# Opening the gated unit by single tiles of tokens: one bank for both turned tiles, groups closed late, gate weights from a second queue

## The chip, the cores and the metric

The kernel runs on one core of a Trainium2 chip. The engines named here are TensorE (PE, with its weight loads listed apart as PEld), VectorE (DVE), ScalarE (ACT), GpSimd (POOL) and SyncE (SP), which in this kernel only issues transfers. The metric is the device time of one execution in microseconds: 184.51 us, the median of three runs (184.46 to 184.68).

## What is computed

The input is 2048 tokens of 448 values, in bfloat16. Each token is normalised over its 448 values. The normalised tokens go two ways.

```
xn   = (x - mean) / sqrt(var + 1e-5)
Bu   = xn @ B_bar^T                       # complex, 448 states
h[t] = Lam_bar * h[t-1] + Bu[t]           # complex recurrence over the tokens
s    = 2 * Re(h @ C^T) + xn * Dskip
g    = silu((sigmoid(xn @ w_gate) * (xn @ w_up)) @ w_down)      # 448 -> 1792 -> 448
out  = x + s * g
```

`B_bar` comes from `Lambda`, `log_dt` and `B`; `w_gate` and `w_up` are 448 x 1792, `w_down` is 1792 x 448.

## The kernel before

The tokens are cut into four chunks of 512 (`TC`), each of four tiles of 128 (`P`); `HC` is 256, half a chunk. The 448 inputs are held transposed in `xnT`, as three whole blocks of 128 rows and a last block of 64. That last block is stored twice, in rows 0 to 63 and 64 to 127, so that the last 64 rows of a gate product and of an up product can run side by side in the two halves of TensorE's rows. The 1792 columns of gate and up are 14 groups of 128 (`ft` 0 to 13). A group of a chunk is a sum of three whole products and one half product, in one PSUM bank for the gate (`g_ps`) and one for up (`u_ps`). The helper `gu_wholes` issues the whole products, `gu_halves` the half ones, over the tokens `n0` to `n1`; `first` says whether these products open the sum or close it.

There are eight PSUM banks. They are given out in turn under one tag (`bank`, 8 buffers): a new tile gets the oldest bank and has to wait until that one's last reader is done.

Chunk 0 is special, since nothing can run before its tokens are there (lines 929 to 1021). TensorE first runs 31 products on a unit matrix (`warm`). VectorE takes the statistics of tiles 0, 1 and 3, ScalarE those of tile 2. POOL takes the power -0.5 of the variance, VectorE normalises (`ln_norm`), a small copy doubles the last 64 columns (VectorE for tiles 0 and 1, POOL for 2 and 3), TensorE turns the tile by four transposes into PSUM (`ln_turn`, line 274), and VectorE copies the turned tile into `xnT` (`ln_out`, line 282). Tiles 0 and 2 are turned into one bank (`tps[0]`), tiles 1 and 3 into another (`tps[1]`).

The opening then takes the first four groups (`gus`) in two halves of the chunk. When tiles 0 and 1 are in `xnT`, the whole gate products of groups 0 to 2 are issued over 256 tokens, then their up products. Tiles 2 and 3 are turned. Then come the half products of groups 0 to 2 for the first 256 tokens, all of group 3 for those tokens, the half products of all four groups for the second 256 tokens, and at last their whole products, group by group. Group 3 uses the two banks of the turned tiles, and so waits for their copies. Between all this VectorE and ScalarE make the tables of sines and cosines for the recurrence (`emit_frac`, `emit_abs`, `emit_sin`, `emit_cos`); then ScalarE takes the tanh of each gate bank (`gu_out`) and VectorE copies each up bank (`up_copy`).

Behind the opening the main stream begins: groups 4 to 13 of chunk 0 and the products of the recurrence's input, and then the other chunks. All of its products are issued by one helper (`Sum.add`, line 510). `keep_order`, called at the end, ties each instruction to the one written before it on its engine: every engine runs its instructions in the order in which the code writes them.

Loads: SP issues nearly all transfers, in written order. At the start these are three loads of tokens of chunk 0 (tile 0, tile 1, tiles 2 and 3 together), then by `load_w(sync, 0, 512)` the first 512 columns of the gate weights, of the up weights, and of the last 64 rows of both (`wt`); then B, more weights and the tokens of chunk 1. ScalarE's queue issues three small rows of vectors before ScalarE's first table load.

Of the kernel before, what the change touches and what calls it, by code (L numbers as in the profile page):

```python
# [11 lines left out]
BF16 = mybir.dt.bfloat16  # L12
# [7 lines left out]
P = 128  # L20
TC = 512
HC = TC // 2
NCH = S_TOK // TC
TPC = TC // P
KT = 4
# [38 lines left out]
def kernel(  # L64
# [52 lines left out]
        eng.dma_start(out=t[:, 0:3, f0:f1], in_=mat[0:384, f0:f1].rearrange("(kt p) f -> p kt f", p=P))  # L117
        eng.dma_start(out=t[0:64, 3, f0:f1], in_=mat[384:448, f0:f1])

    def load_w(eng, f0, f1, between=None):  # L120
        for t, mat in ((wg, B_w_gate), (wu, B_w_up)):
            eng.dma_start(out=t[:, :, f0:f1], in_=mat[0:384, f0:f1].rearrange("(kt p) f -> p kt f", p=P))
        if between:
            between()
        for mat, p0 in ((B_w_gate, 0), (B_w_up, 64)):
            eng.dma_start(out=wt[p0:p0 + 64, f0:f1], in_=mat[384:448, f0:f1])
# [12 lines left out]
    load_row(act, 1, A_Lambda_im)  # L139
    load_row(act, 2, A_Lambda_re)  # L140
    sync.dma_start(out=x_t[0][:, 2:4, :], in_=x_src[:, 2:4, :])
    load_w(sync, 0, 512)
    raw = {}

    def load_x(c):
# [44 lines left out]
    def warm(n):  # L190
        for _ in range(n):
            pe.matmul(warm_ps[:], lhsT=ident[:], rhs=ident[:], start=True, stop=True)
# [74 lines left out]
    def ln_turn(c, j):  # L267
        xb, cols = xn[c % 3], slice(j * P, (j + 1) * P)
        if c > 0:
            sync.dma_start_transpose(out=xnT[c][:, 0:KT, cols], in_=xb[:, j, :])  # L270
            return
        (dve if j < 2 else pool).tensor_copy(out=xb[:, j, D:DP], in_=xb[:, j, 384:D])
        for kt in range(KT):
            pe.transpose(tps[j % 2][:, kt, :], xb[:, j, kt * P:(kt + 1) * P], ident[:])

    def ln_twice(c, copy, j0=0, j1=TPC):
        copy(out=xn[c % 3][:, j0:j1, D:DP], in_=xn[c % 3][:, j0:j1, 384:D])
# [1 line left out]
            ln_turn(c, j)  # L279

    def ln_out(j):
        dve.tensor_copy(out=xnT[0][:, :, j * P:(j + 1) * P], in_=tps[j % 2][:])  # L282

# [403 lines left out]

    def gu_halves(c, ft, gt, ut, first, n0=0, n1=TC):
        f0, f1 = ft * P, (ft + 1) * P
        for t, p0 in ((gt, 0), (ut, 64)):
            pe.matmul(t[:, n0:n1], lhsT=wt[p0:p0 + 64, f0:f1],  # L695
                      rhs=xnT[c][p0:p0 + 64, 3, n0:n1], start=first, stop=not first)

    def gu_wholes(c, ft, gt, ut, first, n0=0, n1=TC, which=(0, 1)):
        f0, f1 = ft * P, (ft + 1) * P
        for t, wm in [((gt, wg), (ut, wu))[i] for i in which]:  # L700
            for kt in range(3):
                pe.matmul(t[:, n0:n1], lhsT=wm[:, kt, f0:f1], rhs=xnT[c][:, kt, n0:n1],  # L702
                          start=(first and kt == 0), stop=(not first and kt == 2))


    def gu_out(ft, gt, ub):
# [229 lines left out]
    ln_root(1, 1)  # L936
    ln_sum(2)
    turn_twice(tp_v, rows, 3)
    tps = [ps.tile([P, KT, P], BF16, name="tp_x", tag="bank", bufs=8) for _ in range(2)]
    ln_norm(0, 0)  # L940
    ln_turn(0, 0)
    emit_vecs()
# [4 lines left out]
    ln_pow_of(2, 1, sums[:, 2:3, 1:2], 1.0 / D)  # L947
    ln_norm(0, 1)
    ln_turn(0, 1)
    warm(5)  # L950
    ln_out(0)
    ln_out(1)
    ln_stats(3)
# [5 lines left out]
    ln_pow_of(3, 1, mv[:, 3:4, 1:2], 1.0)  # L959

    gus = [(bank("g_ps"), bank("u_ps")) for _ in range(3)]
    for ft in range(3):
        gu_wholes(0, ft, *gus[ft], True, 0, HC, (0,))
    for ft in range(3):
        gu_wholes(0, ft, *gus[ft], True, 0, HC, (1,))
    ln_norm(0, 2)
    ln_turn(0, 2)
    emit_frac(0)
    ln_norm(0, 3)
    ln_turn(0, 3)  # L970
    emit_abs(0)
    for j in (2, 3):
        ln_out(j)
    emit_frac(1)
    emit_abs(1)
    emit_frac(3)
    emit_abs(3)
    emit_frac(2)
    emit_abs(2)
    for ft in range(3):  # L980
        gu_halves(0, ft, *gus[ft], False, 0, HC)
    gus.append((bank("g_ps"), bank("u_ps")))
    gu_wholes(0, 3, *gus[3], True, 0, HC)
    gu_halves(0, 3, *gus[3], False, 0, HC)
    for ft in range(4):
        gu_halves(0, ft, *gus[ft], True, HC, TC)
    for ft in range(4):
        gu_wholes(0, ft, *gus[ft], False, HC, TC)
    emit_steps()
    for pt in (0, 1, 3):  # L990
        emit_sin(pt)
# [152 lines left out]
```

## Time and profile before

| | |
|---|---|
| median of three runs | 184.51 us (184.46 to 184.68) |
| profiled execution, its own time | 184.13 us |
| its span, first to last instruction | 182.4 us |
| PE busy | 177.3 us, 97% of the span |
| DVE, ACT, POOL busy | 163.7, 113.7, 25.0 us |
| PE's warm-up products | 1.35 to 4.84 us |
| first gate product of chunk 0 | 6.73 us |
| first product of the main stream (L510) | 13.86 us |

Times in the profile's lines are microseconds from the start of the span. A line of the timeline gives start, length, engine, source line, operation, what it writes and reads, and how many instructions are put together; where an engine stood idle before, a bracket says for how long and what ended it. A line of the chain gives start, length and what held the end of the program there. PEld rows are weight loads, which overlap products. An engine name with a q, as SPq, is its sequencer, which issues transfers. Matmuls are pipelined, so the length of one row holds its latency, and the spacing of starts is what a product costs in a row of them.

### The profile page before, as it was taken

The page shows a single profiled execution, that of the slowest core. Times are in us where ns is not written, and L with a number is a line of the kernel's source. Part 1 is how long each engine was busy: PE and PEld are TensorE (multiplying, and loading weights), DVE is VectorE, ACT ScalarE, POOL GpSimd, SP SyncE. Part 2 cuts the span into 40 slices and gives each one's busy share as a digit, 9 for nine tenths or more (in the row PEclk, how much of TensorE's full clock was granted, in tenths as well). Part 3 has the DMA queues.
Part 4 walks back from the last instruction along what each step waited for, and adds up shares of the span by engine and source line. Part 5 has one row for each costly group of instructions (what it writes and reads, how often), then busy time and mean ns, then how long its engine had stood idle before and what let it go on. Part 6 is the DMA issues. An engine that isn't in the chain of part 4 may idle for free.

```text
span 182.4 us, 4465 instructions
## 1 busy us (share of the span) xinstructions
PE 177.3 (97%) x1701; PEld 104.0 (57%) x1701; DVE 163.7 (90%) x335; ACT 113.7 (62%) x236; POOL 25.0 (14%) x61
## 2 busy tenths in 40 slices
PE   7999999999999999999999999999999999999992
PEld 7776888446654445645654445545665545656552
DVE  4899999799989979999999999699999999699574
ACT  3999677978587787988277665067048657152220
POOL 4768557220000000004000000000000000000000
PEclk9999999999999999999999999999999999999999
DMA  5999997894434113011231010030000000011102
GB/s 154 321 321 276 214 132 120 267 288 97 90 79 86 32 29 101 5 59 43 59 61 29 4 29 0 4 101 0 4 14 16 4 16 15 4 53 51 29 25 76
DMA packets 27659, 15.07 MB, mean 83 GB/s; under 512 B 16243, under 2 KB 27638, under 8 KB 27638
## 3 DMA queue, kind: packets, MB, share of 16 engines
q1 hardware_dynamic: 27632, 14.79, 34.4%
q8 instruction: 13, 0.21, 0.5%
q14 instruction: 8, 0.07, 0.1%
q10 hardware_dynamic: 6, 0.00, 0.0%
HBM read 8.49 MB, written 1.84 MB: 57 GB/s over the span
## 4 chain that ended last, share of the span: by engine, by line
PE 94%; DVE 3%; DMA 1%; POOL 0%; issue 0%; DVEq 0%
PE g_ps L510 25%; PE d_ps L510 23%; PE u_ps L510 19%; PE bu L510 12%; PE y_ps L510 11%; PE g_ps L702 2%; PE u_ps L702 1%; DMA x<-in_A_x_dram 1%; DVE sg L861 1%; PE g_ps L695 1%; DVE xnT L282 0%; DVE xn L261 0%; DVE stats L208 0%; DVE o_l L867 0%; POOL rsd L238 0%
## 5 line engine op out<-in xcount | busy, mean ns | idle before, releaser
L510 PE MATMUL u_ps<-xnT,wu 64*128 64x512 bf16 x312 | 69.1, 376 | 0.0
L510 PE MATMUL g_ps<-xnT,wg 64*128 64x512 bf16 x312 | 61.8, 376 | 0.0
L740 ACT ACTIVATE sig<-g_ps 128x512 bf16<-128x512 f32 x52 | 29.1, 596 | 29.1 <-PE g_ps L510 29.1
L510 PE MATMUL bu<-xnT,bT 64*128 64x512 bf16 x196 | 45.7, 376 | 0.0
L510 PE MATMUL d_ps<-wd,hF 64*128 64x448 bf16 x448 | 43.9, 349 | 0.0
L510 PEld LDWEIGHTS <-hF 64*128 64x128 bf16 x448 | 26.5, 94 | 16.2
L510 PEld LDWEIGHTS <-wu 64*128 64x128 bf16 x312 | 25.8, 94 | 16.7 <-POOLq L512 1.6
L510 PEld LDWEIGHTS <-wg 64*128 64x128 bf16 x312 | 23.1, 94 | 16.3 <-POOLq L512 1.9
L740 ACT CAST ub<-u_ps 128x512 bf16<-128x512 f32 x52 | 29.3, 604 | 0.8 <-DVE hF L712 0.8
L510 PE MATMUL y_ps<-ct,h 64*128 64x448 bf16 (+2 forms) x203 | 22.8, 343 | 0.0
L510 PEld LDWEIGHTS <-bT 64*128 64x128 bf16 x196 | 17.8, 94 | 8.8
L589 DVE TENSOR_TENSOR_SCAN wv<-r_col,st,ta 128x512 bf16<-128x512 f32 x18 | 22.6, 1274 | 0.1
L737 DVE TENSOR_TENSOR hF<-sig,ub 128x512 bf16<-128x512 bf16 x52 | 20.8, 415 | 1.0 <-ACT ub L740 0.8
L510 PE MATMUL g_ps<-xnT,wt 64*128 64x512 bf16 x52 | 19.6, 376 | 0.0
L510 PE MATMUL u_ps<-xnT,wt 64*128 64x512 bf16 x52 | 19.6, 376 | 0.0
L510 PEld LDWEIGHTS <-h 64*128 64x128 bf16 (+1 forms) x203 | 13.3, 95 | 8.2 <-issue 0.4
L570 ACT CAST bus<-bu 128x512 bf16<-128x512 f32 x24 | 14.3, 596 | 2.1 <-PE bu L510 1.9
L768 ACT ACTIVATE sigd<-d_ps 128x448 bf16<-128x448 f32 x12 | 6.6, 549 | 12.3 <-PE d_ps L510 12.3
L238 POOL TENSOR_TENSOR rsd<-ve,mhalf 128x1 f32<-128x1 f32 (+2 forms) x8 | 7.3, 917 | 48.5 <-PE u_ps L510 45.6
L510 PEld LDWEIGHTS <-wt 64*128 64x128 bf16 x104 | 9.8, 94 | 4.9
L832 DVE TENSOR_TENSOR o_t<-y_ps,xn 128x448 bf16<-128x448 f32 x12 | 6.9, 618 | 3.7 <-PE y_ps L510 3.7
L583 DVE TENSOR_TENSOR ta<-ta,tb 128x1024 bf16<-128x1024 bf16 x12 | 8.3, 690 | 0.3
(151 smaller groups left out, 214.7 us busy)
## 6 DMA issues: line engine op xcount, KB each, us to landing
wd<-in_B_w_down_dram SPq DMA_DIRECT2D x1, 1568.0 KB, 7.4
x<-in_A_x_dram SPq DMA_DIRECT2D x3, 448.0 KB, 5.9
out_dram<-o_t SPq DMA_DIRECT2D x6, 224.0 KB, 2.1
wg<-in_B_w_gate_dram SPq DMA_DIRECT2D x2, 384.0 KB, 4.2
wu<-in_B_w_up_dram SPq DMA_DIRECT2D x2, 384.0 KB, 5.3
wg<-in_B_w_gate_dram SPq DMA_DIRECT2D x1, 576.0 KB
wu<-in_B_w_up_dram SPq DMA_DIRECT2D x1, 576.0 KB, 8.0
bsw<-bus SPq DMA_DIRECT2D x8, 64.0 KB, 2.1
```

What stands on the lines that cost most here:

```text
L238: pool.tensor_tensor(out=rsd[:, t:t + n, :], in0=ve[:, t:t + n, :], in1=mhalf[:, 0:n, :], op=ALU.pow)
L510: m = pe.matmul(self.t[:, n0:n1], lhsT=lhsT, rhs=rhs, start=self.done == 1, stop=self.done == self.n)
L570: empty = [lambda cc=cc: act.copy(out=bus[:, cc, :], in_=pst[cc][:]) for cc in range(2)]
L583: dve.tensor_tensor(out=T["ta"][:], in0=T["ta"][:], in1=T["tb"][:], op=add)
L589: dve.tensor_tensor_scan(out=T["wv"][:, cc, :], data0=rb, data1=T["ta"][:, cc, :], initial=(0.0 if c == 0 else st[pt][:, cc, :]), op0=mul, ...
L695: pe.matmul(t[:, n0:n1], lhsT=wt[p0:p0 + 64, f0:f1], rhs=xnT[c][p0:p0 + 64, 3, n0:n1], start=first, stop=not first)
L702: pe.matmul(t[:, n0:n1], lhsT=wm[:, kt, f0:f1], rhs=xnT[c][:, kt, n0:n1], start=(first and kt == 0), stop=(not first and kt == 2))
L737: dve.tensor_tensor(out=h[:], in0=sig[:], in1=ub[:], op=ALU.mult)
L740: u.empty = [lambda: act.activation(sig[:], gt[:], ACT.Sigmoid), lambda: act.copy(out=ub[:], in_=ut[:])]
L768: act.activation(sigd[:], ds[j][:], ACT.Sigmoid)
L832: dve.tensor_tensor(out=o[:, i, :], in0=ys[c, j + 2 * i][:], in1=xb[:, i, :], op=ALU.add)
L861: dve.tensor_tensor(out=sg[:, d0:d1], in0=ys[c, j][:, d0:d1], in1=gs[c][:, j, d0:d1], op=ALU.mult)
```

## The change

- The two turned tiles share one PSUM tile `tps`, one half each, where there were two tiles and two banks.
- The helpers no longer take `first`. A list `opened` remembers which banks have had a product: the first product in a bank opens it (`start`), and only the products marked `last` close it (`stop`).
- The gate products of groups 0 to 2 over the first 256 tokens are issued as two rounds of 128 tokens, tile 0 and then tile 1. The up products stay at 256.
- The gate products of group 3 over the first 256 tokens come ahead of the turn of tile 2, in a bank taken before; the half products of groups 0 to 2 come between the turns of tiles 2 and 3.
- The whole products over tiles 2 and 3 of groups 0 to 2 are issued in 128 tokens each: tile 2 directly behind the turn of tile 3, tile 3 at the end. Group 3's up products over the first 256 tokens follow those of tile 2.
- On VectorE one `emit_frac` moves between the copies of tiles 2 and 3.
- Two of the five warm-up products ahead of the first gate product are left out.
- The first load of gate weights is issued by ScalarE's queue (`first=act`), ahead of ScalarE's first table load.

```diff
--- before.py
+++ after.py
@@ -117,9 +117,9 @@
         eng.dma_start(out=t[:, 0:3, f0:f1], in_=mat[0:384, f0:f1].rearrange("(kt p) f -> p kt f", p=P))
         eng.dma_start(out=t[0:64, 3, f0:f1], in_=mat[384:448, f0:f1])
 
-    def load_w(eng, f0, f1, between=None):
-        for t, mat in ((wg, B_w_gate), (wu, B_w_up)):
-            eng.dma_start(out=t[:, :, f0:f1], in_=mat[0:384, f0:f1].rearrange("(kt p) f -> p kt f", p=P))
+    def load_w(eng, f0, f1, between=None, first=None):
+        for e, t, mat in ((first or eng, wg, B_w_gate), (eng, wu, B_w_up)):
+            e.dma_start(out=t[:, :, f0:f1], in_=mat[0:384, f0:f1].rearrange("(kt p) f -> p kt f", p=P))
         if between:
             between()
         for mat, p0 in ((B_w_gate, 0), (B_w_up, 64)):
@@ -139,7 +139,7 @@
     load_row(act, 1, A_Lambda_im)
     load_row(act, 2, A_Lambda_re)
     sync.dma_start(out=x_t[0][:, 2:4, :], in_=x_src[:, 2:4, :])
-    load_w(sync, 0, 512)
+    load_w(sync, 0, 512, first=act)
     raw = {}
 
     def load_x(c):
@@ -271,7 +271,7 @@
             return
         (dve if j < 2 else pool).tensor_copy(out=xb[:, j, D:DP], in_=xb[:, j, 384:D])
         for kt in range(KT):
-            pe.transpose(tps[j % 2][:, kt, :], xb[:, j, kt * P:(kt + 1) * P], ident[:])
+            pe.transpose(tps[:, j % 2, kt, :], xb[:, j, kt * P:(kt + 1) * P], ident[:])
 
     def ln_twice(c, copy, j0=0, j1=TPC):
         copy(out=xn[c % 3][:, j0:j1, D:DP], in_=xn[c % 3][:, j0:j1, 384:D])
@@ -279,7 +279,7 @@
             ln_turn(c, j)
 
     def ln_out(j):
-        dve.tensor_copy(out=xnT[0][:, :, j * P:(j + 1) * P], in_=tps[j % 2][:])
+        dve.tensor_copy(out=xnT[0][:, :, j * P:(j + 1) * P], in_=tps[:, j % 2])
 
 
 
@@ -689,18 +689,23 @@
 
 
 
-    def gu_halves(c, ft, gt, ut, first, n0=0, n1=TC):
+
+    opened = []
+
+    def gu_product(t, last, **a):
+        pe.matmul(start=not any(o is t for o in opened), stop=last, **a)
+        opened.append(t)
+
+    def gu_halves(c, ft, gt, ut, n0=0, n1=TC):
         f0, f1 = ft * P, (ft + 1) * P
         for t, p0 in ((gt, 0), (ut, 64)):
-            pe.matmul(t[:, n0:n1], lhsT=wt[p0:p0 + 64, f0:f1],
-                      rhs=xnT[c][p0:p0 + 64, 3, n0:n1], start=first, stop=not first)
-
-    def gu_wholes(c, ft, gt, ut, first, n0=0, n1=TC, which=(0, 1)):
+            gu_product(t, False, out=t[:, n0:n1], lhsT=wt[p0:p0 + 64, f0:f1], rhs=xnT[c][p0:p0 + 64, 3, n0:n1])
+
+    def gu_wholes(c, ft, gt, ut, last, n0=0, n1=TC, which=(0, 1)):
         f0, f1 = ft * P, (ft + 1) * P
         for t, wm in [((gt, wg), (ut, wu))[i] for i in which]:
             for kt in range(3):
-                pe.matmul(t[:, n0:n1], lhsT=wm[:, kt, f0:f1], rhs=xnT[c][:, kt, n0:n1],
-                          start=(first and kt == 0), stop=(not first and kt == 2))
+                gu_product(t, last and kt == 2, out=t[:, n0:n1], lhsT=wm[:, kt, f0:f1], rhs=xnT[c][:, kt, n0:n1])
 
 
     def gu_out(ft, gt, ub):
@@ -936,7 +941,7 @@
     ln_root(1, 1)
     ln_sum(2)
     turn_twice(tp_v, rows, 3)
-    tps = [ps.tile([P, KT, P], BF16, name="tp_x", tag="bank", bufs=8) for _ in range(2)]
+    tps = ps.tile([P, 2, KT, P], BF16, name="tp_x", tag="bank", bufs=8)
     ln_norm(0, 0)
     ln_turn(0, 0)
     emit_vecs()
@@ -947,7 +952,7 @@
     ln_pow_of(2, 1, sums[:, 2:3, 1:2], 1.0 / D)
     ln_norm(0, 1)
     ln_turn(0, 1)
-    warm(5)
+    warm(3)
     ln_out(0)
     ln_out(1)
     ln_stats(3)
@@ -959,33 +964,41 @@
     ln_pow_of(3, 1, mv[:, 3:4, 1:2], 1.0)
 
     gus = [(bank("g_ps"), bank("u_ps")) for _ in range(3)]
+    for j in range(2):
+        for ft in range(3):
+            gu_wholes(0, ft, *gus[ft], False, j * P, (j + 1) * P, (0,))
     for ft in range(3):
-        gu_wholes(0, ft, *gus[ft], True, 0, HC, (0,))
-    for ft in range(3):
-        gu_wholes(0, ft, *gus[ft], True, 0, HC, (1,))
+        gu_wholes(0, ft, *gus[ft], False, 0, HC, (1,))
+    g3 = bank("g_ps")
+    gu_wholes(0, 3, g3, None, False, 0, HC, (0,))
     ln_norm(0, 2)
     ln_turn(0, 2)
     emit_frac(0)
+    for ft in range(3):
+        gu_halves(0, ft, *gus[ft], 0, HC)
     ln_norm(0, 3)
     ln_turn(0, 3)
     emit_abs(0)
-    for j in (2, 3):
-        ln_out(j)
+    ln_out(2)
     emit_frac(1)
+    ln_out(3)
+    gus.append((g3, bank("u_ps")))
     emit_abs(1)
     emit_frac(3)
     emit_abs(3)
     emit_frac(2)
     emit_abs(2)
     for ft in range(3):
-        gu_halves(0, ft, *gus[ft], False, 0, HC)
-    gus.append((bank("g_ps"), bank("u_ps")))
-    gu_wholes(0, 3, *gus[3], True, 0, HC)
-    gu_halves(0, 3, *gus[3], False, 0, HC)
-    for ft in range(4):
-        gu_halves(0, ft, *gus[ft], True, HC, TC)
-    for ft in range(4):
-        gu_wholes(0, ft, *gus[ft], False, HC, TC)
+        gu_wholes(0, ft, *gus[ft], False, HC, HC + P)
+    gu_wholes(0, 3, *gus[3], False, 0, HC, (1,))
+    for ft in range(3):
+        gu_halves(0, ft, *gus[ft], HC, HC + P)
+        gu_halves(0, ft, *gus[ft], HC + P, TC)
+    gu_halves(0, 3, *gus[3], 0, HC)
+    gu_halves(0, 3, *gus[3], HC, TC)
+    for ft in range(3):
+        gu_wholes(0, ft, *gus[ft], True, HC + P, TC)
+    gu_wholes(0, 3, *gus[3], True, HC, TC)
     emit_steps()
     for pt in (0, 1, 3):
         emit_sin(pt)
```

## The prediction

> **What bounds the kernel now.** I read the page first, its summary and its chain: who is busy, and whose work ends last.
>
> ```profile
> span 182.4 us, 4465 instructions
> PE 177.3 (97%) x1701; PEld 104.0 (57%) x1701; DVE 163.7 (90%) x335; ACT 113.7 (62%) x236; POOL 25.0 (14%) x61
> ...
> PE 94%; DVE 3%; DMA 1%; POOL 0%; issue 0%; DVEq 0%
> ```
>
> TensorE (PE) carries 94% of the chain. The change touches the first 14 us only, so the question is when PE leaves the opening, the first products of chunk 0, and enters the main stream (L510), which it then works through in a fixed order. The chain in order of time, from the second turned tile of tokens on (start, length, what):
>
> ```profile
> 5.71 0.21 DVE xn L272
> 5.93 0.32 DVE xnT L282
> 6.25 0.00 issue
> 6.25 0.44 DVE xnT L282
> 6.69 0.04 issue
> 6.73 1.14 PE g_ps L702 x9
> 7.87 0.98 PE u_ps L702 x9
> 8.85 0.50 PE tp_x L274 x8
> 9.36 0.21 PE g_ps L695
> ...
> 9.79 0.43 PE g_ps L702 x3
> 10.22 0.33 PE u_ps L702 x3
> ...
> 11.21 0.43 PE g_ps L702 x3
> ...
> 13.93 0.32 PE g_ps L510
> ```
>
> The first products wait for both copies of turned tiles (L282); they start at 6.73. From there to 13.93 PE never pauses: 7.20 us. Two prices stand in it. A product over 256 tokens costs 0.98 / 9 = 0.109 us; eight turns (128 columns each, each with its own weight load) cost 0.50, 0.0625 apiece. Where PE goes from 128-row to 64-row products or back, about 0.10 is lost (0.43 for three products of 0.33 in all); the first product of a stretch after a wait costs some 0.17 of fill (1.14 − 0.98).
>
> The timeline shows what the copies wait for:
>
> ```profile
> 5.74 0.48 PE L274 MATMUL tp_x<-ident,xn 128*128 128x128 bf16 x4
> 6.05 0.44 PE L192 MATMUL warm_ps<-ident 128*128 128x128 bf16 x5
> ```
> ```profile
> 5.84 0.84 DVE L282 COPY xnT<-tp_x 128x512 bf16<-128x512 bf16 x2
> 6.59 0.62 DVE L208 BATCH_NORM_STATS2 stats<-x 128x6 f32<-128x448 bf16 x1
> ```
>
> Tile 1's turn ends at 5.74 + 0.48 = 6.22, but the copy of tile 0 starts at 5.84: today it waits only for its own turn. Tile 1's copy then runs 6.25 to 6.69.
>
> **The change, part by part.**
>
> *One bank for both turned tiles.* In the changed program as it is built, the copy of tile 0 waits for the last turn of tile 1, and the copy of tile 1 has no wait left; likewise the copy of tile 2 waits for the last turn of tile 3. So sharing the tile has a price: copy 0 starts at 6.26 instead of 5.84 and ends at 6.69, when both are done today. Copy 1 ends near 7.05, since two copies in a row take 0.76 to 0.84 together. The first products need only copy 0 now: they start at 6.73, as before. Gain: nothing. On DVE the statistics of tile 3 (6.59) and all behind them slip by about 0.4. Tile 2's normalisation goes from 7.47 to 7.9, POOL's little copy from 8.29 to 8.7; PE wants tile 2 at about 9.3. Tile 3's POOL copy ends near 9.5, PE wants it near 10.1. Both are covered, by 0.4 or more.
>
> *Opening with single tiles.* 9 gate products of 256 columns become 18 of 128. The trace has no such product; the nearest row is the turns, the same shape with a new weight each: 0.0625. Bounds: 0.055 (five warm-up products in 0.44 with a latency of 0.22, so (0.44 − 0.22) / 4) and 0.08 (busy weight loading under the eight turns, 0.64 / 8). I take 0.0625: 18 × 0.0625 − 0.98 = +0.15 (bounds +0.01, +0.46). Tile 1's half starts at 6.73 + 9 × 0.0625 = 7.29, after its copy.
>
> *Tiles 2 and 3 likewise.* 18 products of 256 (groups 0 to 2, gate and up) become 36 of 128: 36 × 0.0625 − 18 × 0.109 = +0.29 (+0.02, +0.92). Six half-row pairs of 128 stand in for three of 256: 0.375 − 0.33 = +0.05 (−0.1, +0.2).
>
> The Trainium skill, TensorE: Matmul & The Clock Gate, section Back-to-back issue gap, gives a sustained 81 ns for weight load and matmul pairs at N = 128, against 62.5 in the row of turns here. By it the three terms would be +0.48, +0.95 and +0.15 in place of +0.15, +0.29 and +0.05. I go by the row.
>
> *The order behind the second half.* Before, eight turns came together and then 1.2 us of other work (6 half products, group 3 on tiles 0 and 1, its halves) lay between them and the first use of tiles 2 and 3, which hid the copies (9.11 to 9.87). After, the gate of group 3 comes ahead of turn 2 and the halves between turns 2 and 3; directly behind turn 3 stand the products of tile 2. They need copy 2, and copy 2 needs the end of turn 3. In time: 18 gate products end at 6.73 + 0.17 + 1.13 = 8.03, 9 up at 9.01, 3 of group 3 at 9.34, turn 2 at 9.59, six halves at 10.02, turn 3 (0.10 + 0.25) at 10.37. Copy: 10.41 to 10.83 (0.42). First product at 10.87, plus 0.17 of fill. PE stands for 0.67 with nothing behind turn 3 that it may do first. Bounds: 0.46 (copy and two semaphore hops of 0.02, no fill) and 0.9 (if an engine upstream is late too). I take +0.67. Copy 3 stands behind one `frac` (0.48): done near 11.7, wanted at 12.0; the up products of group 3, whose bank that copy frees, at 12.2.
>
> *Bank of group 3, and flags.* g3 takes the bank of the small vectors, free since 5.4. Which product clears or closes a bank adds no instruction. Nothing.
>
> *Two warm-up products fewer:* 0.11 in a stretch where PE waits for DVE until 6.73 anyway. Nothing.
>
> *First gate weights from ScalarE's queue.* One issue of about 0.49 goes from SP to ACT. On SP the ten loads behind it move up by 0.5; PE's list of waits names no DMA, so nothing comes of that. On ACT, the table load at 1.81 moves to 2.3 and the dummy ends at 3.8 instead of 3.3; the next thing, the sum of tile 2, waits for its tokens until 4.36. Covered by 0.56. The weights themselves land at 2.11 + 3.7 = 5.8 now and are wanted at 6.73. They are now in flight beside tokens 2 and 3 (landing at 1.64 + 2.7 = 4.34). If the two share the engines evenly, the tokens land about a microsecond later, 5.3: ACT's sum, square and POOL's power slip so that tile 2's normalisation comes near 8.25, its POOL copy ends near 8.9, still before 9.3. Nothing, with 0.3 to 0.4 of margin left.
>
> The Trainium skill, DMA: Bandwidth & Descriptors, section Issuing engines are not separate DMA queues, says that a second issuing engine saves only sequencer time and that the transfers interleave. That speaks against a gain here; nothing in the trace of before shows two large loads from two queues at once.
>
> *Behind the opening.* PE enters L510 about 1.15 later. ACT's first tanh goes from 12.21 to about 13.5, DVE's first up copy from 12.23 to 13.7. The first banks that L510 wants back (g0, g1) are free by 14.1 and 14.6, PE wants them at 15.0. Later PE waits for nothing that a delay could hide: its listed waits behind 14 us are the fixed hops at changes of row half. So the delay stays.
>
> Sum: 0.15 + 0.29 + 0.05 + 0.67 = +1.15 (rounded). The profiled execution took 184.13 around its span of 182.4, 0.38 below the median of 184.51; 184.13 + 1.15 = 185.28 on its own footing, 185.66 on the median's. I say 185.6.
>
> **The rivals.**
>
> *Weight loads set the pace of 128-column products* (0.08 each): 0.46 + 0.92 + 0.15 + 0.67 = +2.2, 186.7. For: 98 ns for one load. Against: turns with the same loads run at 0.0625, as they overlap. 0.14.
>
> *The gate weights land late from the other queue:* if they are served behind the up weights, which land at 2.62 + 4.9 = 7.5, the first products start 0.8 later: +1.9, 186.4. It decides from a landing after 6.7. For: nothing is known of the sharing. Against: 0.9 of margin. 0.12.
>
> *PE's clock falls back* after the stand and the shorter warm-up. The 31 warm-up products took 3.49, 0.113 each, twice the later 0.055, though the granted clock reads 1.00; a slow stretch of some 2 us would cost 1 more: 186.7 or above. Against: PE's thin time from 5.4 to 6.7 brings no such thing. 0.05.
>
> *The delay is taken up later,* in part, by work whose start a DVE wait sets (DVE waits 3.7 us for `y_ps`): +0.5, 185.0. Against: 97% busy PE. 0.09.
>
> *Faster: the copies wait only for their own turn.* Then tile 0's products start at 6.29, and the stand behind turn 3 is gone: 0.15 + 0.29 + 0.05 − 0.44 = +0.05, 184.6, and with products at 0.055 −0.5, 184.0. It decides if copies 0 and 2 start before their neighbour's turn ends. Against: the built waits. 0.05.
>
> **How the numbers follow.** The forecast, +1.15, has 0.55. About 0.2%, 0.37 us, is what a measurement can tell here. Faster: 0.03 from the last rival and 0.01 for the unseen, 0.04. Within: its other 0.02 and 0.04 of the delay taken up, 0.06. Slower: the rest, 0.90. The range reaches from the delay half taken up, 184.9, to the slow products, 186.8.
>
> **What would show it.** Right: first gate product at 6.7, at about 0.06 spacing; the copy of tile 0 starting at 6.26 and not 5.84; PE idle about 0.5 behind the turn of tile 3, put down to DVE `xnT`; L510 from about 15.0. Wrong: gate products waiting for a DMA; a spacing of 0.08 or more; no idle time behind turn 3; L510 at 13.9 or before.

## The result, and the profile after

The changed kernel takes 185.44 us, median of six runs (185.21 to 185.73). The kernel before, on the same chip, takes 184.49 (184.41 to 184.68). The ratio is 1.0048, 95% interval 1.0038 to 1.0059: slower by 0.95 us.

The profiled execution of the changed kernel took 185.56 us, 0.12 above its median. That of before took 184.13, 0.36 below its own. So the two traces differ by 1.43 us, of which 0.48 is the choice of executions. Both numbers are needed below.

The page of the changed kernel, its summary and the engines' shares of its chain:

```profile
span 183.7 us, 4527 instructions
PE 178.0 (97%) x1732; PEld 105.0 (57%) x1732; DVE 163.7 (89%) x335; ACT 113.9 (62%) x236; POOL 24.9 (14%) x61
...
PE 94%; DVE 2%; POOL 1%; issue 0%; POOLq 0%; DVEq 0%
```

PE is still 97% busy, but it has hardly more work: 178.0 against 177.3 us. POOL has come onto the chain, on which it had 0% before. The chain in order of time shows where (start, length, what):

```profile
6.39 0.43 DVE xnT L282
...
6.87 1.28 PE g_ps L696 x18
...
10.11 0.34 PE tp_x L274 x4
...
10.48 0.44 DVE xnT L282
...
10.96 0.33 PE g_ps L696 x3
...
13.59 1.29 DVE ub L1013 x2
14.88 0.14 DVE spm L447
...
15.07 0.63 POOL spm L452
15.70 0.34 POOL cosT L450
16.05 0.56 POOL spm L452
16.60 0.15 POOL cosT L450
...
16.80 0.82 PE g_ps L510 x5
```

Two things are new in it. First, the copy of tile 2 (L282) starts at 10.48, directly behind the turn of tile 3, and PE goes on at 10.96; before, that copy started at 9.11. Second, the chain leaves PE at 13.57, where group 0's up bank is closed, and comes back to it only at 16.80. In between VectorE copies two up banks (L1013), negates a sine table (`emit_neg`, L447), and POOL mirrors tables (L452, L450). VectorE itself came free at 13.57 (its negation of table 0 ran from 13.35 for 0.22), so the late closing of that bank and VectorE's own queue are level there, within about 0.1.

PE did not idle from 13.57 to 16.80. It reached the main stream at 14.81 (13.86 before) and stopped in it, as the timeline of PE shows (a bracket is idle time and what ended it):

```profile
14.81 0.82 PE L510 MATMUL g_ps<-xnT,wg 64*128 64x512 bf16 x6
...
16.80 0.70 PE L510 MATMUL g_ps<-xnT,wg 64*128 64x512 bf16 x4 [0.30 <-POOLq L512]
```

The same two rows, and the pair of copies that begins with tile 2, in the kernel before:

```profile
9.11 0.76 DVE L282 COPY xnT<-tp_x 128x512 bf16<-128x512 bf16 x2
13.86 0.82 PE L510 MATMUL g_ps<-xnT,wg 64*128 64x512 bf16 x6
15.43 0.91 PE L510 MATMUL g_ps<-xnT,wg 64*128 64x512 bf16 x6
```

The second of PE's rows begins with the fifteenth product of the main stream, the first whose sum goes over to the other half of TensorE's rows. `Sum.add` puts an empty POOL instruction there (line 512, `pool.nop()`), which waits for the other half's last product and which the next product waits for. The text calls this instruction POOL's word, and the start of that product G. The word is queued on POOL behind the mirror copies. The list of waits from 14 to 20 us, first of the changed kernel, then of the one before (total, times, longest):

```profile
PEld L510 <- POOLq L512: 0.8, 1, 0.8
PE g_ps L510 <- POOLq L512: 0.3, 1, 0.3
```
```profile
PEld L510 <- POOLq L512: 0.4, 1, 0.4
POOL spm L452 <- DVE spm L447: 0.4, 1, 0.4
```

Before, PE itself has no wait for L512 in the list. The trace gives the word at 15.36 before and at 16.73 after.

The chain runs from VectorE over POOL's mirror copies to the word, but the times name another last step. The last mirror copy in POOL's queue, directly ahead of the word, is that of the sine table 2. It waits for VectorE's negation of this table, which VectorE makes behind all four up copies. Here is the negation, first in the kernel before, then in the changed one:

```profile
14.97 0.35 DVE L447 TENSOR_SCALAR spm<-spm 128x256 bf16<-128x256 bf16 x1
```
```profile
16.34 0.35 DVE L447 TENSOR_SCALAR spm<-spm 128x256 bf16<-128x256 bf16 x1
```

It ends at 15.32 before and at 16.69 after, and the word follows 0.04 later in both. At that moment POOL is still at the copy before the last (15.18 to 15.58 and 16.54 to 16.94), so the word waits neither for that copy's end nor for the last copy to run. In 12 of the 14 executions below the word comes 0.04 behind the end of this negation. The other two are those in which the negation was moved ahead of the last up copies; there the word comes 0.04 behind the end of PE's sixth product in the main stream. So what delays the word is VectorE's queue, and not the length of POOL's copies.

So the trace holds two losses: +0.95 where PE enters the main stream, and +0.42 more at its fifteenth product (16.80 − 15.43 = 1.37). From G on nothing more is lost: 184.13 − 15.43 = 168.70 before and 185.56 − 16.80 = 168.76 after.

### The profile page after: what moved, and what is told of

Same layout as the page of the kernel before. It is cut to its first block, busy times and chain, and to the rows that moved or that the text cites. A ratio compares the mean times of both kernels' runs of the same rounds, so it can differ in the third digit from the quotient of the medians.

```text
span 183.7 us, 4527 instructions
## 1 busy us (share of the span) xinstructions
PE 178.0 (97%) x1732; PEld 105.0 (57%) x1732; DVE 163.7 (89%) x335; ACT 113.9 (62%) x236; POOL 24.9 (14%) x61
## 4 chain that ended last, share of the span: by engine, by line
PE 94%; DVE 2%; POOL 1%; issue 0%; POOLq 0%; DVEq 0%
PE g_ps L510 24%; PE d_ps L510 23%; PE u_ps L510 19%; PE bu L510 12%; PE y_ps L510 11%; PE warm_ps L192 2%; PE g_ps L696 2%; PE u_ps L696 1%; PE tp_x L274 1%; DVE sg L866 1%; DVE ub L1013 1%; POOL spm L452 1%; DVE xnT L282 0%; DVE o_l L872 0%; POOL cosT L450 0%
## 5 line engine op out<-in xcount | busy, mean ns | idle before, releaser
L510 PE MATMUL u_ps<-xnT,wu 64*128 64x512 bf16 x312 | 69.1, 376 | 0.0
L510 PE MATMUL g_ps<-xnT,wg 64*128 64x512 bf16 x312 | 61.8, 376 | 0.3 <-POOLq L512 0.3
L510 PE MATMUL bu<-xnT,bT 64*128 64x512 bf16 x196 | 45.7, 376 | 0.0
L510 PE MATMUL d_ps<-wd,hF 64*128 64x448 bf16 x448 | 43.9, 349 | 0.0
L510 PEld LDWEIGHTS <-hF 64*128 64x128 bf16 x448 | 26.5, 94 | 16.2
L510 PEld LDWEIGHTS <-wu 64*128 64x128 bf16 x312 | 25.8, 94 | 16.7 <-POOLq L512 1.6
L510 PEld LDWEIGHTS <-wg 64*128 64x128 bf16 x312 | 23.1, 94 | 16.7 <-POOLq L512 2.4
L510 PE MATMUL y_ps<-ct,h 64*128 64x448 bf16 (+2 forms) x203 | 22.9, 343 | 0.0
L510 PEld LDWEIGHTS <-bT 64*128 64x128 bf16 x196 | 17.8, 94 | 8.8
L510 PE MATMUL g_ps<-xnT,wt 64*128 64x512 bf16 x52 | 19.6, 376 | 0.0
L510 PE MATMUL u_ps<-xnT,wt 64*128 64x512 bf16 x52 | 19.6, 376 | 0.0
L510 PEld LDWEIGHTS <-h 64*128 64x128 bf16 (+1 forms) x203 | 13.3, 95 | 8.2 <-issue 0.4
L510 PEld LDWEIGHTS <-wt 64*128 64x128 bf16 x104 | 9.8, 94 | 4.8
```

The costliest lines, as they stand in the source:

```text
L510: m = pe.matmul(self.t[:, n0:n1], lhsT=lhsT, rhs=rhs, start=self.done == 1, stop=self.done == self.n)
```

## The experiments

All twelve runs in one table, in microseconds. "Median" is beside the median of the kernel before on the same chip; the ratio is taken over the rounds run beside each other and is not exactly that of the two medians. The last four columns are one profiled execution each: start of the copy of tile 2, entry into the main stream, G, and the execution's own time less G.

| kernel | median / before | ratio (95%) | copy 2 | entry | G | own − G |
|---|---|---|---|---|---|---|
| before | 184.49 | | 9.11 | 13.86 | 15.43 | 168.70 |
| after | 185.44 / 184.49 | 1.0048 (1.0038–1.0059) | 10.48 | 14.81 | 16.80 | 168.76 |
| before, shared bank | 185.17 / 184.50 | 1.0035 (1.0013–1.0056) | 10.10 | 14.72 | 16.63 | 168.70 |
| before, other queue | 184.51 / 184.50 | 0.9990 (0.9973–1.0008) | 9.30 | 14.27 | 15.79 | 168.75 |
| after, old order | 185.35 / 184.50 | 1.0045 (1.0023–1.0068) | 9.70 | 14.37 | 16.23 | 168.74 |
| after, two negations early | 185.25 / 184.50 | 1.0031 (1.0013–1.0050) | 10.24 | 14.56 | 16.42 | 168.75 |
| before, narrow gate rounds | 185.12 / 184.59 | 1.0033 (1.0016–1.0050) | 9.50 | 14.47 | 16.00 | 168.69 |
| after, first table early | 185.81 / 184.59 | 1.0078 (1.0048–1.0109) | 12.24 | 16.57 | 18.85 | 168.76 |
| before, first table early | 185.01 / 184.59 | 1.0023 (1.0008–1.0038) | 9.11 | 13.86 | 16.29 | 168.71 |
| before, one more DVE operation | 185.02 / 184.59 | 1.0014 (1.0002–1.0026) | 9.12 | 13.86 | 16.04 | 168.70 |
| after, all negations early | 184.88 / 184.54 | 1.0017 (1.0006–1.0028) | 10.19 | 14.52 | 16.04 | 168.67 |
| before, all negations early | 184.63 / 184.54 | 1.0000 (0.9987–1.0012) | 9.08 | 13.83 | 15.35 | 169.41 |
| after, two banks | 184.82 / 184.54 | 1.0015 (1.0005–1.0026) | 9.41 | 14.12 | 16.10 | 168.77 |
| after, more PE work | 185.44 / 184.54 | 1.0046 (1.0028–1.0064) | 10.41 | 14.97 | 16.72 | 168.74 |

The last column is the strongest reading of the study. In 13 of the 14 executions it is 168.67 to 168.77, over a range of G of 3.4 us. In ten of them G follows the word by 0.07; in three PE came to G by itself (before with the other queue, before with narrow gate rounds, after with all negations early). The time is set where the fifteenth product starts; the one exception is read below.

### The parts alone: the shared bank and the queue

The kernel before, with only the turned tiles in one bank:

```diff
-            pe.transpose(tps[j % 2][:, kt, :], xb[:, j, kt * P:(kt + 1) * P], ident[:])
+            pe.transpose(tps[:, j % 2, kt, :], xb[:, j, kt * P:(kt + 1) * P], ident[:])
...
-    tps = [ps.tile([P, KT, P], BF16, name="tp_x", tag="bank", bufs=8) for _ in range(2)]
+    tps = ps.tile([P, 2, KT, P], BF16, name="tp_x", tag="bank", bufs=8)
```

> The kernel before, with nothing changed but that both turned tiles share one bank. Theory (the waits of the shared bank and the order cost the time): copy 0 waits for the turn of tile 1, starts near 6.3 instead of 5.84, and copy 1 ends near 7.05 instead of 6.69; the first products, which here need both copies, start near 7.1; +0.35 against before, 184.85. Rival N (the narrow products cost the time): no narrow product here, so no change, 184.5. Rival Q (the load from the other queue and the shorter warm-up cost it): neither is here, 184.5.

Measured: ratio 1.0035, +0.67 by the medians, two thirds of the whole loss and more than was expected. The timeline of its VectorE gives the two places:

```profile
6.43 0.76 DVE L282 COPY xnT<-tp_x 128x512 bf16<-128x512 bf16 x2 [0.32 <-PE tp_x L274]
10.10 0.76 DVE L282 COPY xnT<-tp_x 128x512 bf16<-128x512 bf16 x2 [0.42 <-PE tp_x L274]
```

Both pairs of copies start only when the second turn of their pair is done. The products of 256 tokens need both copies, so PE starts at 7.24 here, 0.51 later than before. That part the changed kernel does not pay, since its first round needs one tile only. The second pair is late in both.

The kernel before with the gate weights on ScalarE's queue and two warm-up products fewer:

```diff
-    load_w(sync, 0, 512)
+    load_w(sync, 0, 512, first=act)
...
-    warm(5)
+    warm(3)
```

> The kernel before, with nothing changed but the first gate weights issued by ScalarE's queue and three warm-up products in place of five. Theory: covered, 184.5, within 0.1 of before; tokens 2 and 3 land up to 1 us later and nobody waits longer for it. Rival Q: most of the 0.95 is here, 185.0 to 185.4, and the first products start later than 6.73 for a slower clock of PE. Rival N: 184.5.

Measured: ratio 0.9990, interval across 1. No cost and no gain. In its profiled execution the chain does show the weights ending last ahead of the first product:

```profile
1.82 4.97 DMA wg<-in_B_w_gate_dram
...
6.84 0.39 PE g_ps L702 x2
```

They took 4.97 us there and 3.9 in the changed kernel's own trace. At 6.84 the first product was 0.1 late, and the copies of tiles 0 and 1 were done by 6.61 there, so the margin was used up in this execution. In the eight executions with the other queue these weights took 3.9 to 5.0 us, and the tokens of tiles 2 and 3 took 2.9 to 3.7 us (2.7 to 2.9 with all loads on SP). That scatter does not show in the median.

### Is it the order behind the second half?

The changed kernel, with the work behind the second half in the order of before (shared bank, narrow products and loads as changed):

```diff
-    g3 = bank("g_ps")
-    gu_wholes(0, 3, g3, None, False, 0, HC, (0,))
...
-    for ft in range(3):
-        gu_halves(0, ft, *gus[ft], 0, HC)
...
+    for ft in range(3):
+        gu_halves(0, ft, *gus[ft], 0, HC)
+    gus.append((bank("g_ps"), bank("u_ps")))
+    gu_wholes(0, 3, *gus[3], False, 0, HC)
```

> The changed kernel with the second half of the opening in the order of before (turns of tiles 2 and 3 together, then group 3 and the half products), all its narrow products kept, one bank, the loads as changed. Theory: no stand behind the turn of tile 3 and the up banks close group by group as before, so the word that POOL passes on in the main stream is not late; left are the narrow products (18 at 0.0617, 36 at 0.0555: +0.15 in all), 184.65. Rival N: all 54 narrow products are still there, so still near 185.4. Rival Q: the loads are still as changed, 185.4.

Measured: ratio 1.0045, as slow as the changed kernel. The theory that PE's stand behind turn 3 alone makes the loss fell here. PE has other work behind the turn in this order and enters the main stream at 14.37, 0.44 earlier than the changed kernel. (The profiled execution was the fastest of twelve, 0.38 below the median, so its places are early ones.) But G is at 16.23, held by POOL's word: PE alone would have come there at 14.37 + 1.52 = 15.89, with the 1.52 that is worked out below. Its chain goes from the turn of tile 3 to the copies and then along VectorE's tables, the up copies and POOL, not along PE.

### Is it VectorE's queue and POOL's word?

The changed kernel with the negations of tables 1 and 3 ahead of the up copies:

```diff
         emit_cos(pt)
-        if pt == 0:
-            emit_neg(pt)
+        emit_neg(pt)
...
-            emit_neg(1)
-            emit_neg(3)
```

> The changed kernel, with two small VectorE instructions (the sign change of the sine tables 1 and 3, emit_neg) moved ahead of the first two up copies, so that POOL's table copies, and the word queued behind them, do not wait for the up copies. Theory (the late closing of the up banks reaches PE by way of VectorE and POOL): the hold at the change of halves at 16.8 goes, 0.4 to 0.5 less than the changed kernel, 185.0. Rival (the hold is the fixed hop, and the delay is that of the opening alone): no change, 185.4.

Measured: ratio 1.0031; 0.75 slower than before by the medians where the changed kernel is 0.95. That is the direction expected and half the size, and the interval overlaps that of the changed kernel, so this run alone does not tell them apart. The negation of table 2 still stood behind all four up copies: it ended at 16.31, POOL had run out of copies at 16.21, and the word came at 16.35 (16.73 in the changed kernel).

Taking that negation ahead of the last two up copies as well:

```diff
             emit_anf()
+            emit_neg(2)
             emit_step_sines()
-    emit_neg(2)
```

> The changed kernel with VectorE's sign changes of tables 1 and 3 ahead of the first two up copies and that of table 2 ahead of the last two, that of table 0 where it was. Chain theory (POOL's word waits for the table copies and for the last sign change on VectorE): the word at about 16.1, level with TensorE's own 16.1 to 16.3, instead of 16.73; -0.4 to -0.6 against the changed kernel, 184.9 to 185.0. TensorE theory: no change, 185.4.

Measured: ratio 1.0017, +0.34 by the medians in place of +0.95. The word came at 15.38 and PE no longer waits for it. Its chain:

```profile
10.19 0.44 DVE xnT L282
...
10.67 0.33 PE g_ps L696 x3
...
16.20 0.86 PE g_ps L510 x7
```

The stand behind turn 3 is still there (10.19 to 10.67), and PE runs from it through G without a pause. Moving three small VectorE operations, none of which feeds a product of the opening, took away 0.6 of 0.95. That the word, and VectorE's queue behind it, decides the changed kernel's time is thereby shown. What is left, about 0.3, is put down to PE's own way, as PE's chain runs unbroken from the stand to G; no run removes that rest by itself.

The same move in the kernel before:

> The kernel before with the same three sign changes moved up. Chain theory: the word comes at 14.9 to 15.1 and no longer holds TensorE, which goes on by itself at 15.4; little is won where both were level, more in executions in which the loads came late: -0.1 to -0.2, 184.3 to 184.4, faster than both kernels. TensorE theory: no change, 184.5.

Measured: ratio 1.0000. The word came at 14.69 and G moved a little, to 15.35, but the time did not follow; this is the one execution whose own time less G is not 168.7. The list of waits of this run (14 to 24 us) names DMAs that no list of before or after names there:

```profile
PEld L510 <- DMA bT<-b_im: 0.5, 1, 0.5
...
PE bu L510 <- DMA bT<-b_im: 0.2, 1, 0.2
```

The chain of this run follows the transposing transfer of `bT` until 21.08. SP was busy issuing it for 3.05 us there (2.16 in the kernel before, 2.64 in the changed one), and the edit touches none of the transfers. Whether that is the next limit in every execution of this kernel, one trace cannot say. The gain that was expected did not come.

The cost of VectorE time in the kernel before, measured by itself: one more table operation, which writes a slot that nothing reads before it is overwritten, directly behind the copies of tiles 2 and 3.

```diff
         ln_out(j)
+    dve.scalar_tensor_tensor(out=ct[:, 0, 0:HC], in0=iota_f[:], scalar=K["turn"][:, 0:1], in1=iota_f[:],
+                             op0=ALU.mult, op1=ALU.subtract)
     emit_frac(1)
```

> The kernel before with one more VectorE instruction behind the copies of tiles 2 and 3, a multiply-subtract of 128x256 like frac (0.48), whose output nobody reads. Chain theory (from the copy of tile 2 on, VectorE's table work, its up copies, POOL's table copies and the word behind them set when the main stream goes on, 6.25 to 6.46 after that copy's start in all six traces so far, and TensorE in its opening is only level with it): the word at about 15.8 instead of 15.36, +0.4, 184.9. TensorE theory (as in the prediction: TensorE's own products set the opening, VectorE has room there): no change, 184.5.

Measured: ratio 1.0014, +0.43 by the medians, for an operation of 0.48 (0.39 on the chain). The interval of the ratio, 1.0002 to 1.0026, is 0.04 to 0.48 us, so the sign is clear and the size is not. PE enters the main stream at 13.86 to the hundredth as before, and loses the time only at G:

```profile
13.86 0.82 PE L510 MATMUL g_ps<-xnT,wg 64*128 64x512 bf16 x6
...
16.04 0.91 PE L510 MATMUL g_ps<-xnT,wg 64*128 64x512 bf16 x6 [0.49 <-POOLq L512]
```

So in the kernel before, VectorE's queue behind copy 2 had no slack either. PE alone would have come to G at 13.86 + 1.52 = 15.38 (1.52 is what the stretch takes where nothing holds it: 16.04 − 14.52 with all negations early, 15.79 − 14.27 with the other queue), and by the word G stood at 15.43: two paths that end within 0.05 us of each other. From copy 2 to the word it is 6.25 in before (15.36 − 9.11), 6.25 in after (16.73 − 10.48) and 6.37 here without the added 0.48 (15.97 − 9.12). The range that the expectation gave for all six earlier traces, 6.25 to 6.46, holds for five; where two negations were early it was 6.11 (16.35 − 10.24).

The counterpart, 8 products of 64 columns more on PE in the changed kernel (they add zeros to a bank):

```diff
         gu_wholes(0, ft, *gus[ft], True, HC + P, TC)
+    for _ in range(8):
+        gu_product(gus[3][0], False, out=gus[3][0][:, 0:64], lhsT=ident[:], rhs=raw["b_re"][:, 0, D:DP])
```

> The changed kernel with eight more products on TensorE, 64 columns of zeros each with its own weight load, ahead of the last products of group 3, behind the closing of groups 0 to 2: about 0.4 of TensorE time. Chain theory (in the changed kernel TensorE has about 0.45 to spare between the opening and POOL's word): the main stream starts about 0.4 later, goes on where it did, and the time stays within 0.1 of 185.4. TensorE theory: +0.4, 185.8.

Measured: ratio 1.0046 and a median of 185.44, that of the changed kernel to the hundredth. The eight products took 0.24 (13.98 to 14.22), less than the 0.4 meant; PE enters the main stream at 14.97, 0.16 later than the changed kernel, and G stands at 16.72:

```profile
16.53 0.15 POOL cosT L450
...
16.72 0.82 PE g_ps L510 x5
```

So 0.24 of PE time ahead of G cost nothing in the changed kernel, while VectorE time moved the word in both kernels.

### Two tries to shorten the word's path further

The first table's sine, cosine and negation moved up to the copies of tiles 2 and 3, in the kernel before and in the changed one (negations 1 and 3 early as well):

```diff
     emit_abs(0)
+    emit_sin(0)
+    emit_cos(0)
+    emit_b_twice()
     for j in (2, 3):
         ln_out(j)
+    emit_neg(0)
     emit_frac(1)
```

> The kernel before with the sign changes of the sine tables moved up on VectorE: that of table 0 directly behind the copies of tiles 2 and 3, those of 1 and 3 ahead of the first up copies, so that POOL's table copies run earlier; ScalarE's order is as before. Chain theory: the word no longer holds TensorE, which then goes on by itself at about 15.4: 0.0 to -0.1 in an execution where both are level, 184.4. TensorE theory: no change, 184.5. They part in the next kernel, not here; this one is its measure.

> The changed kernel with the same sign changes moved up. Chain theory: the word is early enough (under 16.0), TensorE goes on at 14.8 + 1.5 = 16.3 instead of 16.8: -0.4 to -0.5 against the changed kernel, 185.0; what is left against before, about +0.5, is TensorE's own: the stand behind the turn of tile 3 and the narrow first products. TensorE theory: no change, 185.4.

Measured: 1.0023 and 1.0078, both slower, where no loss or a gain was expected. In the kernel before the reason can be read. POOL's mirror copies of the first table now run from 10.65 on, while VectorE makes the next tables, and VectorE's operations became longer (0.29 and 0.48 for the same two lines before):

```profile
10.67 0.52 DVE L430 TENSOR_SCALAR afrac<-frac 128x256 int32<-128x256 int32 x1
11.11 0.82 DVE L424 SCALAR_TENSOR_TENSOR frac<-iota_f,turn,whole 128x256 f32<-128x256 f32 x1
```
```profile
10.99 0.67 POOL L452 COPY spm<-spm 128x510 bf16<-128x510 bf16 x1
```

With the operations moved ahead of it, VectorE comes to the up copies at 13.32 (12.23 before), and the word is at 16.22. POOL's copies ahead of the last one were done at 15.19 there, 1.0 earlier; the negation of table 2 ended at 16.18.

The changed kernel's profiled execution lay 1.8 above its median, with copy 2 only at 12.24, so its places are not compared; one of its table operations took 0.83. Its first gate products show why it was slow:

```profile
7.38 2.08 PE L696 MATMUL g_ps<-xnT,wg 128*128 128x128 bf16 x18 [0.20 <-DVE xnT L282]
```

The same 18 products took 1.28 in the changed kernel's trace and 1.17 in six others. Here they came 0.107 apart, not 0.056, and the up products behind them 0.213 apart in place of 0.109, until about 10.2; the granted clock reads 1.00 throughout.

### The bank taken out of each kernel

The kernel before with the two gate rounds of 128 tokens and the late closing, but with two banks and the old order:

```diff
+    for j in range(2):
+        for ft in range(3):
+            gu_wholes(0, ft, *gus[ft], False, j * P, (j + 1) * P, (0,))
     for ft in range(3):
-        gu_wholes(0, ft, *gus[ft], True, 0, HC, (0,))
...
+        gu_wholes(0, ft, *gus[ft], False, 0, HC, (1,))
```

> The kernel before with its two banks, its loads and its order, but the first gate products in two rounds of 128 tokens, each bank opened once and closed once: the opening by single tiles without the shared bank. The first products need the copy of tile 0 alone, which does not wait for the turn of tile 1: they start near 6.4 instead of 6.73. Chain theory: the copy of tile 2 cannot start before its turn, which waits for POOL's copy (8.53) and then for the products in front of it, so it starts at 9.0 to 9.1 as before and nothing is won: 184.4 to 184.5. TensorE theory: 0.35 won at the start less 0.15 for narrow products: 184.3.

Measured: ratio 1.0033, a miss of half a microsecond to the slow side. In its profiled execution (184.69) the copy of tile 0 came at 6.26 although it waits for its own turn only, copy 2 at 9.50, and the power for tile 2 (POOL) ended at 8.95. Statistics and normalisation ahead of them were late, since the loads of the first two tiles took 2.4 us (median of the two; 2.1 in the kernel before), and the edit touches no load. That explains this execution and not the median. The changed kernel with two banks, below, has the same narrow rounds and loses 0.28 in all, so the rounds do not cost half a microsecond in every order; what they cost in this one stays open.

The changed kernel with two banks for the turned tiles. For want of a bank the gate products of group 3 then move behind those of tile 2, so this is not the bank alone:

```diff
+    tps = [ps.tile([P, KT, P], BF16, name="tp_x", tag="bank", bufs=8) for _ in range(2)]
...
-    g3 = bank("g_ps")
-    gu_wholes(0, 3, g3, None, False, 0, HC, (0,))
...
-    gu_wholes(0, 3, *gus[3], False, 0, HC, (1,))
+    gu_wholes(0, 3, *gus[3], False, 0, HC)
```

> The changed kernel with its two turned tiles in two banks again; for want of a bank the gate products of group 3 go behind those of tile 2. All else is as changed: single tiles, halves between the turns, loads, narrow products. Chain theory: the copy of tile 2 waits for its own turn and starts near 9.4 instead of 10.48, the word follows 6.3 later at 15.7, TensorE does not stand behind the turn of tile 3: 184.7 to 184.9. Rival (the new order and the narrow products cost the time, whatever the banks): 185.3 to 185.4.

Measured: ratio 1.0015, +0.28 by the medians in place of +0.95. The copies no longer wait for their neighbours, and PE does not stand behind turn 3:

```profile
9.77 0.33 PE tp_x L274 x4
10.10 0.17 PE g_ps L696 x3
...
12.90 1.29 DVE ub L1011 x2
...
14.38 0.63 POOL spm L452
```

Copy 2 starts at 9.41, 1.07 earlier than in the changed kernel, the up copies 0.69 earlier, G 0.70 earlier. The chain still goes over POOL. Two other waits come up instead:

```profile
9.11 0.23 PE L274 MATMUL tp_x<-ident,xn 128*128 128x128 bf16 x1 [0.33 <-POOL xn L272]
12.90 1.29 DVE L1011 TENSOR_SCALAR ub<-u_ps 128x512 bf16<-128x512 f32 x2 [0.22 <-PE u_ps L696]
```

PE stands 0.33 for POOL's small copy of tile 2, whose tokens took 3.66 us to land beside the gate weights of the other queue (2.7 in the kernel before). VectorE stands 0.22 for group 0's up bank, which closes late. So the loads and the late closing, which cost nothing where copy 2 is late, have a price where it is not. The bank (with the move it forces) is worth 0.67 of the 0.95, by the difference of the medians' losses, as much as it cost when put into the kernel before by itself. The parts do not add up, though: bank alone 0.67, narrow rounds alone 0.53, both and the rest 0.95. No kernel tried was faster than before.

## Why the prediction was right, and where its working was not

The time and the sign came as forecast: 185.44 for 185.6, inside the range. The working was right in its largest term. It priced the narrow products too high and left out the word, and that these two errors nearly offset each other is luck.

- **First products (T0 at 6.73): right within an execution's scatter.** 6.87 here. The copy of tile 0 waited for the turn of tile 1, as said, and started at 6.39 for 6.26. In five other executions with the shared bank the same copy started at 6.20, 6.21, 6.26, 6.43 and 6.43 (and at 6.90 in the one that lay 1.8 above its median), so the 0.13 is within what one execution differs from another.
- **18 narrow gate products (+0.15): right in this execution, by luck.** 1.28 − 1.14 = +0.14. But 0.11 of it lies in the first five products, two of which came 0.107 behind the one before; the others are 0.056 apart. In six other executions the 18 took 1.17, which is +0.03: the term is mis-sized like the next one.
- **36 narrow products of tiles 2 and 3 (+0.29): mis-sized.** Three of them take 0.17 on the chain, 0.0555 each, the lower bound of the estimate: 36 × 0.0555 − 18 × 0.109 = +0.04. The six half pairs cost nothing: 0.055 each, 0.33, as three wide ones did. The row taken as nearest, the turns at 0.0625, was too dear: seven of the eight turns came 0.056 apart, and the last came 0.10 behind the seventh, just after POOL's copy for tile 3 ended (8.83 + 0.24 = 9.07), so the row holds a wait. The 81 ns of the Trainium skill, TensorE: Matmul & The Clock Gate, section Back-to-back issue gap, would have given +0.95 for this term. The trace disagrees with that figure; it agrees with the N/2.4 + 2.5 ns which the same section has for the isolated gap, 55.8 ns.
- **PE's stand behind the turn of tile 3 (+0.67): right.** Turn done at 10.46, next product at 10.96, and the first three took 0.33 in place of 0.17: 0.50 + 0.17 = 0.67. The mechanism is the one named: one tile for both turns, so that copy 2 waits for turn 3.
- **Entry into the main stream (from 15.0): 14.81.** +0.14 for T0, +0.14 for the narrow gate products and +0.67 for the stand make the whole +0.95; the rest of the opening comes out at nothing.
- **Behind the opening "PE waits for nothing that a delay could hide: its listed waits behind 14 us are the fixed hops at changes of row half": wrong.** The first of these hops is no fixed cost. It is an entry in POOL's queue, behind a mirror copy that waits for VectorE's last negation, and in the trace of before it already set G, 0.05 behind where PE alone would have been. The list of before had `PEld L510 <- POOLq L512: 0.4` and `POOL spm L452 <- DVE spm L447: 0.4` side by side, and its chain showed PE alone, as the two paths ended within 0.05 us of each other. The delay of copy 2 therefore went two ways, and the longer one is not PE's: copy 2 is 1.37 later, the word is 1.37 later, G is 1.37 later.
- **DVE's slip "covered, by 0.4 or more": wrong for the second pair of copies.** The cover was worked out for the operations ahead of the turns. Behind copy 2 there was none: 0.48 more on VectorE cost 0.43 by the medians (0.04 to 0.48 by the interval) without touching PE's entry.
- **The delay stays: right**, from G on, at 168.7 in 13 of 14 executions.
- **Queue, warm-up products, ScalarE (nothing): right by the median**, 0.9990. The margin of 0.9 was overrated: the weights took 3.9 us in one trace and 4.97 in another, where they ended last; and with two banks PE stood 0.33 for tile 2, whose tokens landed at 5.30, the late landing that the prediction had worked out and held covered. The Trainium skill, DMA: Bandwidth & Descriptors, section Issuing engines are not separate DMA queues, agrees with the missing gain.
- **The rivals.** Copies that wait for their own turn only: excluded by the places of copies 0 and 2. Products at 0.08: excluded, 0.0617 and 0.0555 on the mean. Weights late by 0.8: not seen. A clock that falls back: not seen behind the stand; but in one profiled execution of fourteen the wide spacing of products lasted until about 10.2 (5.3 in the kernel before), and it lay 1.8 above its kernel's median, so a slow stretch of that price does occur. Delay taken up later: not seen.

Why the sum still came out: at G the trace has +1.37 for the +1.15 of the sum, since the word's +0.42 more than makes up for the narrow products of tiles 2 and 3 and the half pairs, −0.30. On the medians it is +0.95, because the profiled execution of before was an early one: with 168.7 behind G, its median of 184.49 puts an ordinary G near 15.8, not 15.43. The footing used, "0.38 below the median" added to the result, took that gap to be there after the change too; it was not. That an early G of before is one in which both paths happen to be early fits this, but there is no second trace of before, so it stays argued.

## What to carry to other kernels

In this program two producers' halves in one PSUM tile made the reader of the first half wait for the writer of the second; look at what stands behind that reader on its own engine, not only at who needs its data. The word passed through a third engine came no earlier than the waits of what that engine's queue held ahead of it, so such a word is a path of its own, to be summed from its last waiting instruction. Where the chain shows one engine at 94%, look for a wait on it that ended at the same moment as its own work: an operation added to the other path shows whether that path is level. And before a row's mean is taken as a price, look at the spacing inside the row, for it may hold a wait or a slow start.

## What the runs showed of the hardware

- Products over 128 columns, each with its own weight load, ran at 0.0555 us apiece in rows of three, the spacing of the five warm-up products too. The row of 18 had the same spacing in six executions (1.17 in all); in the changed kernel's trace it took 1.28, with two gaps of 0.107 near its start.
- The same four turns took 0.48 us in one execution and 0.61 in another, with the granted clock at 1.00 in both. In a third the four took 0.61 again, and the products in a row up to about 10.2 us came 0.107 (128 columns) and 0.213 (256 columns) apart, twice the later spacing, also at a granted clock of 1.00. A TensorE that came to its full rate later would look like this; the clock column does not show it.
- VectorE's 32-bit table operations and POOL's bf16 copies lengthen each other when they overlap: 0.48 became 0.82 and 0.29 became 0.52 on VectorE, while in the kernel before POOL's copy (L450) took 0.65 beside them for 0.40 alone. The Trainium skill, SBUF — State Buffer, section Who interferes with whom, has VectorE and GpSimd share a port pair that one of them holds for a whole instruction; the traces agree that either engine may be the one that waits, and do not show the port itself.
- An instruction that does no work on POOL was issued 1.37 us later because the copy ahead of it on that queue waited for VectorE, though the copy before that was still running when it was issued; PE stood 0.30 for it with 97% of its span busy.
